# Warm-up matmuls and the order of the first loads in a fused attention and gated-MLP kernel

## The chip, the cores and the metric

The kernel runs on one core of a Trainium2 chip. A core has a matrix engine (TensorE, PE in the profile; its loading of stationary weights is shown as PEld), VectorE (DVE), ScalarE (ACT), GpSimd (POOL) and SyncE (SP), each with an instruction stream of its own, and 16 DMA engines. DMAs are issued by an engine's instruction stream, here SyncE's, GpSimd's and, for a few, ScalarE's; a stream issues in order, and an instruction that has to wait holds everything behind it in that stream. Times are device microseconds (us). The metric is the median time of one execution; lower is better.

## The reference

The input x has 2048 tokens of 512 numbers in bf16. The output is x + s * g: s is an attention block with 32 heads over cached keys and values, g a gated MLP, both fed with the layer-normalized x.

```python
q = (xn @ wq).reshape(B, Sq, H, Dh).transpose(0, 2, 1, 3)
scores = jnp.einsum("bhqd,bhkd->bhqk", q, k_cache) * (Dh ** -0.5)
p = softmax(scores, axis=-1)
o = jnp.einsum("bhqk,bhkd->bhqd", p, v_cache)
s = o.transpose(0, 2, 1, 3).reshape(B, Sq, H * Dh) @ wo

h = gelu(layernorm(xn) @ w1)        # then four column groups shifted by 1, -1, 2, -2 tokens
x1 = xn + shifted(h) @ w2
g = silu(x1 + gelu(layernorm(x1) @ w3) @ w4)
```

H is 32, Dh 128, and there are 2048 cached keys for each head.

## The kernel before, in words

The tokens are handled as 16 tiles of 128, and the attention as 512 units: for each group of four heads, for each of four blocks of 512 queries, for each head of the group. A unit has eight steps; step n is slot n % 8 of unit n // 8. In a slot TensorE multiplies two chunks of 128 keys with the 512 queries (`s_slot`), ScalarE takes the exponential of the 128 x 1024 result, and TensorE multiplies the exponentials of an earlier slot, four or more behind, with V (`pv_slot`). Between these stand the q projections of a unit two ahead (`q_mm`, `q_copy`), the output projections, and the MLP's matmuls in small pieces. VectorE adds up the exponentials for the softmax's denominator, copies and normalizes. Every instruction is pinned to program order, so the order of the calls in the code is the order on each engine's stream.

Keys come transposed by the DMA: `load_k` loads a head's keys in four pieces (KSPLIT) of 512 keys, each one transposing DMA on SyncE's queue. `load_v` loads a head's V in two halves of 256 KB, `load_w` a head's 128 KB of query weights, `ln1_load` a token tile of 128 KB. The layer norm of a token tile takes statistics (`ln1_stats`, VectorE and two GpSimd instructions), the normalizing (`ln1_apply`, VectorE) and a transpose into xnT (`ln1_turn`, a transposing DMA on SyncE's queue). Tiles 0 to 3 go another way: `first_stats` and `first_tokens` normalize them and turn them on TensorE with the identity matrix, make the first queries, and make the first two key pieces' scores in halves, before the loop over the steps begins at step 4.

What stands ahead of `first_tokens` sets the start-up (lines 799 to 815): four token tiles on SyncE's and ScalarE's queues, query weights of heads 0 to 2 on GpSimd's, head 0's keys and V and head 1's keys on SyncE's, then `warm_up`, which multiplies the identity matrix by itself WARM times into a PSUM tile that nothing reads, while the first tokens arrive. Head 3's weights, token tiles 4 to 7 and head 1's V are issued on GpSimd's queue, and two of head 2's key pieces on SyncE's.

Later loads are put into a table by step with `at(n, fn)`; a step's entries run at the end of the step, in the order in which they were entered. Lines 816 to 830 hold those of the start: for each token tile from 4 on the steps of its statistics, its normalizing and its transpose; the rest of the keys of heads 2 and 3 and the V of head 3 on SyncE's queue; and the V of head 2 at steps 3 and 4 on GpSimd's. The transposed tiles 4 to 7 are first read by `q_mm` of unit 4 at step 22 (line 888). The sums of the early units go through a small DRAM tile on SyncE's queue too (`recip`, `bcast`: dr and rb).

Of the kernel before, what the change touches and what calls it, by code (L numbers as in the profile page):

```python
# [17 lines left out]
def kernel(  # L18
# [15 lines left out]
    nc = tc.nc  # L34
    P = nc.NUM_PARTITIONS
# [15 lines left out]
    HG = 4 if H % 4 == 0 else (2 if H % 2 == 0 else 1)  # L51
# [4 lines left out]
    KSPLIT = 4  # L56
# [1 line left out]
    BASE = 16  # L58
    SHIFT = [1, -1, 2, -2]
    PADW = 32  # L60
    WARM = 48
    PSUM = bass.MemoryType.PSUM
    pin = tc.keep_in_program_order

# [18 lines left out]
    ident = const.tile([P, P], BF16, name="ident")  # L83
# [39 lines left out]
    def mm(out, lhsT, rhs, start, stop):  # L123
        mm_count[0] += out.shape[-1] / 512
        pin(nc.tensor.matmul(out=out, lhsT=lhsT, rhs=rhs, start=start, stop=stop))  # L125
# [6 lines left out]
    def again(t):  # L132
        vn = smp.tile([P, 1], FP32, tag="ve", name="vn")
        var = mv1[t][:, 1:2]
        if t < 4:
            pin(nc.gpsimd.tensor_scalar(out=vn[:], in0=var, scalar1=-EPS, scalar2=None, op0=ALU.add))
            var = vn[:]
        pin(nc.gpsimd.tensor_tensor(out=vn[:], in0=var, in1=rs1[t][:], op=ALU.mult))
        pin(nc.gpsimd.tensor_tensor(out=vn[:], in0=vn[:], in1=rs1[t][:], op=ALU.mult))
        rsqrt(mv1[t][:, 1:2], vn[:])  # L140
# [16 lines left out]
    def at(n, fn):  # L157
        todo[n].append(fn)
# [9 lines left out]
    def load_k(h, pieces):  # L168
        w = Sk // KSPLIT
        for i in pieces:  # L170
            if i == 0:
                kTs[h] = kp.tile([P, Sk], BF16, name="kT")
            pin(nc.sync.dma_start(
                out=kTs[h][:, i * w:(i + 1) * w],
                in_=A_k_cache[0, h, i * w:(i + 1) * w, :], transpose=True))

    def load_v(h, halves, eng=nc.sync):
        v = A_v_cache[0, h].rearrange("(i p j) d -> p i j d", p=P, j=KJ)
        for i in halves:
            if i == 0:  # L180
                vBs[h] = vp.tile([P, KC, Dh], BF16, name="vb")
            ks = slice(i * KSPLIT // 2, (i + 1) * KSPLIT // 2)
            pin(eng.dma_start(
                out=vBs[h].rearrange("p (i j) d -> p i j d", j=KJ)[:, ks], in_=v[:, ks]))

    def load_w(h, eng=nc.sync):
        wqs[h] = wqp.tile([P, DC, Dh], BF16, name="wq_h")
        pin(eng.dma_start(out=wqs[h][:], in_=wq_v[:, :, h * Dh:(h + 1) * Dh]))
# [217 lines left out]
    def ln1_load(t, eng):  # L406
        xin = tokp.tile([P, D], BF16, tag="ta", bufs=6, name="xin")
        pin(eng.dma_start(out=xin[:], in_=xsrc[t]))
        ln[t] = xin

    def ln1_stats(t):
        xin = ln[t]
        bn = smp.tile([P, nc.vector.BN_STATS_DIM], FP32, name="bn")
        pin(nc.vector.bn_stats(out=bn[:], in_=xin[:]))
        pin(nc.vector.bn_aggr(out=mv1[t][:], in_=bn[:]))
        rsqrt(rs1[t][:], mv1[t][:, 1:2])
# [44 lines left out]
    def ln1_apply(t):  # L461
        xns[t] = ln1_norm(t)

    def ln1_turn(t):
        pin(nc.sync.dma_start_transpose(out=xnT[:, :, t * P:(t + 1) * P], in_=xns.pop(t)[:]))

    def warm_up(n):
        wt = psS.tile([P, 2, 512], FP32, name="ps_s")
        for _ in range(n):
            mm(wt[:, 0, 0:P], ident[:], ident[:], True, True)  # L470

    def first_tokens(xns):
        ps = [psX.tile([P, 512], FP32, tag=tag, name="ps_q") for tag in ("xa", "xm")]
# [326 lines left out]
        ln1_load(t, eng)  # L800
    act1 = const.tile([P, 1], FP32, name="act1")
    pin(nc.scalar.activation(out=act1[:], in_=nhalf[:, 0:1], func=ACT.Identity))
    for h in range(HG - 1):
        load_w(h, nc.gpsimd)
    load_k(0, range(KSPLIT))
    load_v(0, (0, 1))
    load_k(1, range(KSPLIT))
    warm_up(WARM)
    xns_0 = first_stats()
    load_w(HG - 1, nc.gpsimd)  # L810
    for t in range(4, 8):
        ln1_load(t, nc.gpsimd)
    first_tokens(xns_0)
    load_v(1, (0, 1), nc.gpsimd)
    load_k(2, (0, 1))
    tokens = ((2, 6, 7), (5, 9, 11), (8, 12, 13), (11, 13, 14),
              (26, 29, 29), (27, 31, 31), (33, 36, 36), (35, 39, 39),
              (37, 45, 45), (47, 53, 53), (55, 61, 61), (63, 69, 69))
    for t, (stats, apply, turn) in enumerate(tokens, 4):
        if t >= 8:  # L820
            at({11: 24, 12: 25}.get(t, stats - 8), lambda t=t: ln1_load(t, nc.gpsimd))
        at(stats, lambda t=t: ln1_stats(t))
        at(max(apply + 1, 28 + 7 * t), lambda t=t: again(t))
        at(apply, lambda t=t: ln1_apply(t))
        at(turn, lambda t=t: ln1_turn(t))
    for n, load, h, piece in ((2, load_k, 2, 2), (4, load_k, 2, 3), (8, load_k, 3, 0), (11, load_k, 3, 1),
                              (15, load_k, 3, 2), (17, load_k, 3, 3), (18, load_v, 3, 0), (20, load_v, 3, 1)):
        at(n, lambda load=load, h=h, piece=piece: load(h, (piece,)))
    for i in range(2):
        at(3 + i, lambda i=i: load_v(2, (i,), nc.gpsimd))  # L830
    for t in range(4):
        at(30 + 3 * t, lambda t=t: again(t))
    at(28, ph1_load)
# [3 lines left out]
    for g in range(NG - 1):  # L837
        b = (g * QT + QT - 1) * HG
        for hh in range(HG):
            h = (g + 1) * HG + hh  # L840
            for i in range(KSPLIT):
                n = (b - 2 + (2 * hh + i // 2 + (hh > 0))) * SPU + (5, 7)[i % 2]
# [32 lines left out]
    for n in range(NS):  # L875
        u, p = divmod(n, SPU)
# [54 lines left out]
        if p == 6 and wo_box:  # L931
            gg, t = wo_todo.popleft()
# [54 lines left out]
    gg, t = wo_todo.popleft()  # L987
# [16 lines left out]
    gg, t = wo_todo.popleft()  # L1004
# [60 lines left out]
```

## Time and profile before

| What | Before |
|---|---|
| Median of three runs | 1246.61 us (1246.46 to 1247.11) |
| Profiled execution | 1245.84 us |
| Its span, first to last instruction | 1244.0 us |
| TensorE busy | 1238.1 us (100% of the span) |
| ScalarE busy | 1128.5 us (91%) |
| VectorE busy | 1117.1 us (90%) |
| GpSimd busy | 175.3 us (14%) |

In a row of the timeline the first number is the start in microseconds from the span's start, the second how long the row lasts, then come the engine, the source line, the operation, the tiles it writes and reads, the shape and the number of instructions merged into the row. "SPq" and the like are a queue's issues of DMAs, not the transfers. A bracket at the end tells the idle time before the row and what ended it. Busy matmul time includes the pipeline, so neighbouring matmuls overlap and a busy TensorE isn't one that streams without a gap. Matmuls and weight loads of all kinds carry line 125, that of the helper `mm`, so tiles tell them apart: ps_q are query projections, ps_s scores, ps_o products with V.

### The profile page before, as it was taken

What the parts mean: (1) busy time and instruction counts of PE and PEld (TensorE: products, weight loads), DVE (VectorE), ACT (ScalarE), POOL (GpSimd) and SP (SyncE); (2) the same over time, 40 slices, a digit from 0 to 9 for tenths busy, and PEclk for the clock granted to TensorE, in tenths of its full rate; (3) what the DMA queues carried; (4) which work ended last, traced back from release to release, by engine and by line L of the source; (5) the groups of instructions that cost most, each with busy time, mean ns of one, the idle gap of its engine ahead of it and who ended that gap; (6) DMA issues with size and microseconds to landing.
All of it is one profiled execution on the core that took longest, in us unless ns stands there. A gap on an engine that the chain in (4) does not pass through costs nothing.

```text
span 1244.0 us, 16647 instructions
## 1 busy us (share of the span) xinstructions
PE 1238.1 (100%) x5816; PEld 597.8 (48%) x5816; DVE 1117.1 (90%) x1521; ACT 1128.5 (91%) x1284; POOL 175.3 (14%) x301
## 2 busy tenths in 40 slices
PE   9999999999999999999999999999999999999998
PEld 5444444444444444444444444444444444444444
DVE  7999999999999988899988889999888999888998
ACT  8999998888999888899998889998888999988992
POOL 6563003432111000000100000010000000000110
PEclk9999999999999999999999999999999999999999
DMA  9565563665624455233483235724346233552463
GB/s 199 126 114 101 106 140 77 127 128 121 143 67 107 107 102 119 52 93 74 108 147 93 69 77 110 132 76 82 85 98 127 56 89 65 123 145 73 108 150 108
DMA packets 248404, 131.42 MB, mean 106 GB/s; under 512 B 200000, under 2 KB 224960, under 8 KB 248320
## 3 DMA queue, kind: packets, MB, share of 16 engines
q1 hardware_dynamic: 238752, 103.94, 39.7%
q0 software_dynamic: 8992, 25.96, 9.4%
q8 instruction: 45, 0.74, 0.3%
q10 hardware_dynamic: 576, 0.46, 0.1%
q14 instruction: 39, 0.32, 0.1%
HBM read 83.62 MB, written 8.13 MB: 74 GB/s over the span
## 4 chain that ended last, share of the span: by engine, by line
PE 97%; DMA 1%; ACT 1%; DVE 1%; issue 0%; SPq 0%; POOL 0%; ACTq 0%; POOLq 0%
PE ps_s L125 36%; PE ps_o L125 35%; PE ps_m L125 10%; PE ps_q L125 9%; PE ps_wo L125 8%; DMA rb<-dr 1%; ACT pT L222 0%; DMA xnT<-xn 0%; DMA dr<-rc 0%; DVE oT L305 0%; ACT xnT L492 0%; ACT pre L595 0%; DVE sm L276 0%; DVE sq L562 0%; DVE acc L233 0%
## 5 line engine op out<-in xcount | busy, mean ns | idle before, releaser
L222 ACT ACTIVATE pT<-ps_s 128x1024 bf16<-128x1024 f32 x1020 | 1020.7, 1029 | 89.7 <-PE ps_s L125 75.6
L125 PE MATMUL ps_s<-qT,kT 128*128 128x512 bf16 (+1 forms) x2056 | 609.1, 378 | 0.1
L125 PE MATMUL ps_o<-pT,vb 128*128 128x512 bf16 x2048 | 607.4, 379 | 0.0
L125 PEld LDWEIGHTS <-kT 128*128 128x128 bf16 x2056 | 232.5, 113 | 226.1 <-issue 1.4
L233 DVE TENSOR_TENSOR acc<-acc,pT 128x2048 bf16<-128x2048 bf16 x256 | 310.5, 1213 | 15.2 <-ACT pT L222 14.5
L125 PEld LDWEIGHTS <-vb 128*128 128x128 bf16 x2048 | 200.2, 98 | 225.5
L228 DVE TENSOR_TENSOR acc<-pT 128x2048 bf16<-128x2048 bf16 x128 | 156.2, 1220 | 31.7 <-ACT pT L222 31.2
L125 PE MATMUL ps_q<-xnT,wq_h 128*128 128x512 bf16 (+1 forms) x524 | 152.8, 374 | 1.1 <-DMA xnT<-xn 0.8
L125 PE MATMUL ps_wo<-wo_h,oT 128*128 128x512 bf16 (+1 forms) x460 | 135.1, 377 | 0.0
L305 DVE TENSOR_TENSOR oT<-ps_o,rb 128x512 bf16<-128x512 f32 x122 | 130.8, 1072 | 2.0 <-DMA rb<-dr 1.8
L391 DVE TENSOR_TENSOR s_acc<-ps_wo,s_acc 128x512 f32<-128x512 f32 x96 | 66.1, 688 | 42.2 <-PE ps_wo L125 41.9
L237 DVE TENSOR_TENSOR acc<-acc 128x1024 bf16<-128x1024 bf16 x128 | 87.5, 684 | 0.3
L276 DVE TENSOR_REDUCE sm<-accT 128x4 f32<-128x512 bf16 x122 | 82.8, 678 | 0.5 <-DMA accT<-acc 0.5
L125 PEld LDWEIGHTS <-wq_h 128*128 128x128 bf16 x524 | 50.7, 98 | 60.6 <-DMA xnT<-xn 1.3
L208 DVE CAST qT<-ps_q 128x512 bf16<-128x512 f32 x109 | 74.9, 688 | 3.9 <-PE ps_q L125 3.6
L125 PE MATMUL ps_m<-xn2T,w_sb 128*128 128x512 bf16 x224 | 77.1, 379 | 0.0
L125 PE MATMUL ps_m<-w_sb,h2T 128*128 128x512 bf16 x224 | 77.1, 379 | 0.0
L727 POOL DMA_DIRECT2D w_sb<-in_B_w_dram x28 | 21.2, 756 | 371.9 <-PE ps_m L125 337.7
L125 PEld LDWEIGHTS <-oT 128*128 128x128 bf16 x468 | 45.7, 98 | 54.3 <-DVE oT L312 0.3
L755 POOL DMA_DIRECT2D g_d<-xr x16 | 8.8, 548 | 438.0 <-DVE xr L753 438.0
L238 DVE TENSOR_TENSOR acc<-acc 128x512 bf16<-128x512 bf16 x128 | 54.4, 425 | 4.4
L554 DVE SCALAR_TENSOR_TENSOR sq<-sq,pre 128x1024 bf16<-128x1024 bf16 x36 | 44.0, 1221 | 4.3 <-ACT sq L550 4.3
(103 smaller groups left out, 638.4 us busy)
## 6 DMA issues: line engine op xcount, KB each, us to landing
rb<-dr SPq DMA_DIRECT2D x127, 256.0 KB, 3.7
vb<-in_A_v_cache_dram SPq DMA_DIRECT2D x60, 256.0 KB, 3.9
w_sb<-in_B_w_dram POOLq DMA_DIRECT2D x28, 256.0 KB, 4.3
wo_h<-in_A_wo_dram SPq DMA_DIRECT2D x32, 128.0 KB, 3.6
wq_h<-in_A_wq_dram SPq DMA_DIRECT2D x28, 128.0 KB, 3.3
kT<-in_A_k_cache_dram SPq DMA_TRANSPOSE x128, 3.7
dr<-rc SPq DMA_DIRECT2D x128, 2.0 KB, 2.1
xr<-in_A_x_dram POOLq DMA_DIRECT2D x16, 128.0 KB, 3.2
```

The lines of the kernel that those rows point to most:

```text
L125: pin(nc.tensor.matmul(out=out, lhsT=lhsT, rhs=rhs, start=start, stop=stop))
L208: pin(nc.vector.tensor_copy(out=qT[:], in_=st[u].pop("psq")[:]))
L222: pin(nc.scalar.activation(out=s["pT"][-1][:, jj:jj + 2, :], in_=sps[:], func=ACT.Exp, scale=SCALE))
L228: pin(nc.vector.tensor_tensor(out=s["acc"][:], in0=s["pT"][0][:], in1=s["pT"][1][:], op=ALU.add))
L233: pin(nc.vector.tensor_tensor(out=a[:], in0=a[:], in1=st[u]["pT"][i][:], op=ALU.add))
L237: pin(nc.vector.tensor_tensor(out=a[:, 0:2, :], in0=a[:, 0:2, :], in1=a[:, 2:4, :], op=ALU.add))
L238: pin(nc.vector.tensor_tensor(out=a[:, 0, :], in0=a[:, 0, :], in1=a[:, 1, :], op=ALU.add))
L276: pin(nc.vector.tensor_reduce(out=sm[:], in_=s.pop("at")[:], axis=mybir.AxisListType.X, op=ALU.add))
L305: pin(nc.vector.tensor_tensor(out=oTs[(g, qt)][:, hh, :].rearrange(f, j=4), in0=s["o"].rearrange(f, j=4), in1=s["rb"].rearrange("x (p j) - ...
L391: pin(nc.vector.tensor_tensor(out=sa, in0=ps[:], in1=sa, op=ALU.add))
L554: pin(nc.vector.scalar_tensor_tensor(out=sq[:].rearrange(f2), in0=sq[:].rearrange(f2), scalar=1.0, in1=pre[:].rearrange(f2), op0=ALU.add, ...
L727: pin(nc.gpsimd.dma_start(out=w[:], in_=w3_v[:, :, fc * P:(fc + 2) * P]))
```

## The change

The warm-up becomes 12 matmuls of the identity with a moving operand of 512 columns (the identity four times over, by a broadcast access). Query weights of heads 1 and 2 move from GpSimd's queue to SyncE's, between head 0's key pieces. Head 1's V moves from GpSimd's queue to SyncE's, its halves between and behind head 1's key pieces. Token tile 7's load moves from the start to step 3, behind tile 4's statistics on GpSimd's queue, and tile 6's behind `first_tokens` in program order. Head 2's V moves from steps 3 and 4 to steps 6 and 9, behind the statistics of tiles 5 and 6. The second key piece of head 3 moves from step 11 to step 14, behind tile 7's transpose.

```diff
-    WARM = 48
+    WARM = 12
...
         for _ in range(n):
-            mm(wt[:, 0, 0:P], ident[:], ident[:], True, True)
+            mm(wt[:, 0, :].rearrange("p (a b) -> p a b", a=4), ident[:],
+               ident[:].unsqueeze(1).broadcast_to([P, 4, P]), True, True)
...
-    for h in range(HG - 1):
-        load_w(h, nc.gpsimd)
-    load_k(0, range(KSPLIT))
+    load_w(0, nc.gpsimd)
+    load_k(0, (0, 1))
+    for h in range(1, HG - 1):
+        load_w(h)
+        load_k(0, (h + 1,))
     load_v(0, (0, 1))
-    load_k(1, range(KSPLIT))
+    for i in range(2):
+        load_k(1, (2 * i, 2 * i + 1))
+        load_v(1, (i,))
     warm_up(WARM)
     xns_0 = first_stats()
     load_w(HG - 1, nc.gpsimd)
-    for t in range(4, 8):
+    for t in range(4, 6):
         ln1_load(t, nc.gpsimd)
     first_tokens(xns_0)
-    load_v(1, (0, 1), nc.gpsimd)
+    ln1_load(6, nc.gpsimd)
     load_k(2, (0, 1))
...
-        if t >= 8:
-            at({11: 24, 12: 25}.get(t, stats - 8), lambda t=t: ln1_load(t, nc.gpsimd))
+        if t >= 7:
+            at({11: 24, 12: 25}.get(t, max(stats - 8, 2)), lambda t=t: ln1_load(t, nc.gpsimd))
...
-    for n, load, h, piece in ((2, load_k, 2, 2), (4, load_k, 2, 3), (8, load_k, 3, 0), (11, load_k, 3, 1),
+    for n, load, h, piece in ((2, load_k, 2, 2), (4, load_k, 2, 3), (8, load_k, 3, 0), (14, load_k, 3, 1),
...
     for i in range(2):
-        at(3 + i, lambda i=i: load_v(2, (i,), nc.gpsimd))
+        at(6 + 3 * i, lambda i=i: load_v(2, (i,), nc.gpsimd))
```

## The prediction

> **What bounds the kernel now.** I read the page's head and its chain of waits first. The profiled execution took 1245.84 us, 1.84 us more than its span; the median of the three runs shown is 1246.61, so what I work out as a difference in the span is put on 1246.61.
>
> ```profile
> span 1244.0 us, 16647 instructions
> PE 97%; DMA 1%; ACT 1%; DVE 1%; issue 0%; SPq 0%; POOL 0%; ACTq 0%; POOLq 0%
> ```
>
> TensorE carries 97% of the chain. The change touches loads and warm-up before the steady state, so only idle time near the start can be won. Stretches of 5 us and one of 18 us show where it is; after the time come PE, PEld, DVE, ACT and POOL busy, then granted clock, DMA share and GB/s:
>
> ```profile
> 5.00:10.00 5.00, 4.72 (x55) 4.09 (x54) 3.25 (x10) 3.52 (x8) 4.76 (x9) 1.00 1.11 183
> 12.50:30.50 18.00, 17.95 (x89) 8.37 (x87) 16.40 (x28) 18.00 (x20) 10.77 (x15) 1.00 1.09 204
> 30.00:35.00 5.00, 4.19 (x20) 1.78 (x18) 3.45 (x5) 3.55 (x5) 0.00 (x0) 1.00 0.73 143
> ```
>
> From 12.5 to 30.5 us both ScalarE (18.00 of 18.00) and TensorE are full and the DMA engines are over 100% booked. Between 30 and 35 us TensorE loses 0.81 us and ScalarE is idle as well. The timelines of these two engines and the chain of waits name the cause:
>
> ```profile
> 29.85 0.59 PE L125 MATMUL ps_o<-pT,vb 128*128 128x512 bf16 x2
> 31.26 0.60 PE L125 MATMUL ps_q<-xnT,wq_h 128*128 128x512 bf16 x2 [0.81 <-DMA xnT<-xn]
> 32.33 1.95 ACT L222 ACTIVATE pT<-ps_s 128x1024 bf16<-128x1024 f32 x2 [1.16 <-PE ps_s L125]
> 28.06 3.16 DMA xnT<-xn
> ```
>
> The q matmul of the second 512 tokens needs token tiles 4 to 7 transposed (xnT). Tile 7's transpose is issued at 28.06 and lands at 31.22; TensorE was ready at 31.26 - 0.81 = 30.45. ScalarE's gap of 1.16 is longer than TensorE's 0.81, so a recovered stall isn't simply swallowed by a busy ScalarE. That 0.81 us is the only DMA wait of any size in the start-up, and the stake of the change. Why is the transpose so late? SyncE's own timeline, all rows up to it (start, time, operation):
>
> ```profile
> 1.65 5.13 SPq L173 DMA_TRANSPOSE kT<-in_A_k_cache_dram  x4
> 6.82 1.09 SPq L183 DMA_DIRECT2D vb<-in_A_v_cache_dram  x2
> 7.96 12.82 SPq L173 DMA_TRANSPOSE kT<-in_A_k_cache_dram  x8
> 20.89 1.22 SPq L465 DMA_TRANSPOSE xnT<-xn  x1
> 22.16 1.26 SPq L173 DMA_TRANSPOSE kT<-in_A_k_cache_dram  x1
> 23.52 1.21 SPq L465 DMA_TRANSPOSE xnT<-xn  x1
> 24.77 1.26 SPq L173 DMA_TRANSPOSE kT<-in_A_k_cache_dram  x1
> 26.13 0.52 SPq L263 DMA_DIRECT2D dr<-rc  x1
> 26.75 2.54 SPq L465 DMA_TRANSPOSE xnT<-xn  x2
> ```
>
> SyncE issues without a pause from 1.65 to 29.3, so its queue, not the data, makes tile 7 late: four key pieces take 5.13 (1.28 each), but the eight from 7.96 take 12.82 where 8 x 1.28 = 10.26 would do. Those 2.56 us of stretched issue fall where the DMA engines are overbooked; I call what is left of them after the change S.
>
> **The change, part by part.** *SyncE's queue.* Added ahead of tile 7's transpose: two query-weight loads and the second head's V in two pieces. Taken from ahead of it: one key piece of head four (step 11 to 14, now behind the transpose of tile 7). Rows for a SyncE weight issue (min/median/max) and the V pair above:
>
> ```profile
> L188 SPq DMA_DIRECT2D wq_h<-in_A_wq_dram x28: 426/526/587, 86.1 to 1042.3; - x28
> DMA to landing us min/median/max: 3.2/3.7/4.1
> ```
>
> Added: 2 x 0.53 + 2 x 0.55 = 2.15 us. Removed: the key piece from 24.77 to the next issue at 26.13, 1.36 us. So tile 7's transpose is issued at 28.06 - 2.56 + S + 2.15 - 1.36 = 26.29 + S. The second row above is the landing time of the four xnT transposes, median 3.7: landing at 29.99 + S against a need at 30.45, so the stall is S - 0.46, and nothing below S = 0.46.
>
> *POOL's queue.* Its rows, and landing medians by queue up to 40 us:
>
> ```profile
> 1.35 2.43 POOL L188 DMA_DIRECT2D wq_h<-in_A_wq_dram  x3 [0.28 <-issue]
> 7.67 2.15 POOL L408 DMA_DIRECT2D xin<-in_A_x_dram  x4
> 9.82 1.43 POOL L183 DMA_DIRECT2D vb<-in_A_v_cache_dram  x2
> 16.02 1.51 POOL L183 DMA_DIRECT2D vb<-in_A_v_cache_dram  x2
> 18.95 0.99 POOL L130 TENSOR_TENSOR rs<-ve,nhalf 128x1 f32<-128x1 f32 x1
> vb<-in_A_v_cache_dram POOLq DMA_DIRECT2D x4, 256.0 KB, 6.8
> xin<-in_A_x_dram POOLq DMA_DIRECT2D x9, 128.0 KB, 4.6
> ```
>
> S comes from here. POOL's loads issued between 6.8 and 17.6 us are one weight tile, four token tiles and four V pieces: 128 + 4 x 128 + 4 x 256 = 1664 KB, in flight beside the eight stretched key pieces. The change takes the second head's V off this queue, holds the third head's until after token tile 5's and tile 6's statistics, and leaves tile 7 in the same stretch, about 16 us: only weights and tiles 4 to 6, 512 KB, are left beside the eight keys before that, 31%. S is bounded by 0 (the stretch was POOL's traffic alone) and 2.56 (it belongs to SyncE's own transposes). As an estimate I scale with the bytes: 0.31 x 2.56 = 0.79, nearer to 0, because SyncE's first four key pieces show no stretch while POOL had only the three weight tiles out. The stall is then 0.79 - 0.46 = 0.33 and the gain 0.81 - 0.33 = 0.48 us.
>
> The Trainium skill (DMA: Bandwidth & Descriptors, "Issuing engines are not separate DMA queues") says that all issuing queues end on the same 16 engines, and that spreading issues only saves sequencer time. By that rule the move saves no transfer and only lengthens SyncE's issue, S stays at 2.56 and the time would be the first rival's. The same page ("SWDGE vs HWDGE vs iDMA") says that GpSimd's loads need descriptors that VectorE's two-port mode can lock out, and SyncE's don't; by that one S is 0 and the whole 0.81 comes back. Between them only the run decides; that the stretch sits at 8 to 21 us and not before speaks for the second.
>
> *Loads that move to where they could be late.* Each is costed at nothing, with its cover:
>
> ```profile
> 9.24 0.82 PE L125 MATMUL ps_q<-xnT,wq_h 128*128 128x128 bf16 x6
> 11.20 0.59 PE L125 MATMUL ps_q<-xnT,wq_h 128*128 128x512 bf16 x2
> 12.96 0.59 PE L125 MATMUL ps_o<-pT,vb 128*128 128x512 bf16 x2
> vb<-in_A_v_cache_dram SPq DMA_DIRECT2D x4, 256.0 KB, 4.2
> kT<-in_A_k_cache_dram SPq DMA_TRANSPOSE x1, 5.3
> DMA to landing us min/median/max: 2.4/3.4/5.9
> 21.00 0.69 DVE L414 BATCH_NORM_STATS2 bn<-xin 128x6 f32<-128x512 bf16 x1
> 23.87 0.41 DVE L449 TENSOR_SCALAR xn<-xin,mv,rs 128x512 bf16<-128x512 bf16 x1 [0.46 <-POOL rs L130]
> 27.98 0.59 PE L125 MATMUL ps_o<-pT,vb 128*128 128x512 bf16 x2
> DMA to landing us min/median/max: 3.1/5.4/9.2
> ```
>
> Head one's query weights take SyncE's third place, issued at 1.65 + 2 x 1.28 = 4.21, needed at 9.24 + 4 x 0.056 = 9.46. The key piece issued in that place took 5.3 (9.51, 0.05 late); weight loads over the whole run take 2.4 to 5.9 with median 3.4 (7.6; at worst 10.1, 0.65 late). Two of three weight loads that shared the DMA engines then have left POOL's queue, so I take the earlier side: no cost. Head two's follow 0.53 + 1.28 = 1.8 us later for a matmul at 11.20, 1.7 later: the same answer. The first V, now issued 2 x 0.53 later at 7.88, has 12.96 - 7.88 = 5.1 us where SyncE's V loads took 4.2.
>
> Tile 7's load leaves at about 16.0 on POOL (where the V pair stood) instead of some 9.3, and is read by the statistics at 21.00: 16.0 + 4.6 = 20.6 is in time, with V's 6.8 it is 22.8, and VectorE waits 1.8. Queued behind that wait are unit 0's reciprocal, unit 1's first sum and the tile's own normalizing, now done at 23.87 + 0.41 = 24.28 and then at 26.1 at the latest: still before SyncE gets to its transpose at 26.29 + S. No cost; SyncE's queue is the cover.
>
> The third head's V is issued after POOL's rs at 19.94; landing 3.1 to 9.2 later (23.0 to 29.1), first read at 27.98: at worst 1.1 late, with the median 6.8 on time by 1.2. No cost.
>
> *Warm-up.* Twelve matmuls of 512 columns replace 48 of 128, the same 6144 columns.
>
> ```profile
> 1.39 5.17 PE L125 MATMUL ps_s<-ident 128*128 128x128 bf16 x48 [1.39 <-DVE ident L87]
> 6.40 0.61 PE L125 MATMUL ps_o<-ident,xn 128*128 128x128 bf16 x8
> 5.28 0.81 ACT L442 ACTIVATE xn<-xin,nb,rsA 128x512 bf16<-128x512 bf16 x1
> ```
>
> The 48 start one per 107 ns until shortly before their end, the eight behind them one per 56 ns: half rate, then full rate, though the clock column says 1.00 at once. Twelve wide ones at half rate take 12 x 4 x 107 = 5.1 us, at full rate 12 x 216 = 2.6 us; if the full rate comes at the same moment, they end where the 48 did. The first token tile is ready at 6.09, so an earlier end wins at most 0.31 and a wholly slow one costs 0.1. I take 0.
>
> **Sum.** -0.48 + 0 + 0 = -0.48 us: 1246.61 - 0.48 = 1246.1 us.
>
> **The rivals.** *SyncE becomes the bound (slower).* S stays 2.56: landing at 32.55, stall 2.10, 1.29 more than now: 1247.9. Decides from S = 0.46 + 0.81 = 1.27. For it: the pure issue time ahead of tile 7 grows by 0.79. Against it: the stretch began only with POOL's V and tokens in flight.
> *A new wait instead.* The third head's V lands at 29.1: TensorE waits 1.1 at step 20, which hides the old wait behind it: 1246.61 - 0.81 + 1.1 = 1246.9. For it: 9.2 is the longest row of that tile. Against: the longest was queued behind other loads.
> *The change doesn't do what it says.* Tile 7's wait stays 0.8, because landing rather than issue grew: 1246.6.
> *The clock rises later.* If the wide warm-up doesn't bring full rate by 6.4, the matmuls up to 9.24 (some 2.5 us of busy time) take twice as long: 1249.1. Against: the same columns stream without a gap.
>
> **How the numbers follow.** Forecast (S between 0 and 1.27, 1245.8 to 1246.6): 0.62. SyncE bound 0.16, new wait 0.08, unchanged 0.09, clock 0.05. The range reaches from 1245.1 (whole stall gone, 0.31 of the warm-up, and 0.4 for the scatter, the three runs shown being 0.65 apart) to 1248.0 (SyncE's full stretch); its own part for the forecast is 1245.6 to 1246.8. A measurement of this kernel can tell about 0.2% (2.5 us) from no change. Faster by that much would need more than every idle stretch of the start: 0.02. Slower by that needs the late clock, or S above 3.8: 0.05. Within: 0.93.
>
> **What would show it.** Right: the wait before ps_q at step 22 shrinks from 0.81 to 0.3 or goes, SyncE's key issues run near 1.28 each, tile 7's transpose is issued near 27.1, the first exponential of step 4 starts as before. Wrong: key issues stretched as now; a wait on wq_h near 9.5, on vb near 28, or on xn before the transpose; more than two matmuls at half rate after the warm-up.

## The result, and the profile after

| What | Before | After |
|---|---|---|
| Median, both on one chip | 1245.85 us (1244.76 to 1247.11, 17 runs) | 1248.17 us (1246.63 to 1251.26, 17 runs) |
| Ratio after / before | | 1.0021, 95% interval 1.0014 to 1.0027 |
| Profiled execution | 1245.84 us | 1246.63 us |
| Its span | 1244.0 us | 1244.9 us |

The change makes the kernel about 2.3 us slower. The forecast was 1246.1, so it missed by 2.1 us, with the wrong sign. One thing has to be kept in mind with every profile below: single executions of one kernel lie up to 4.6 us apart here, and the profiled execution of the changed kernel is the fastest of its 17. It shows where the change begins to cost, not the whole of the median's 2.3 us.

SyncE's timeline of the changed kernel, the rows ahead of tile 7's transpose that answer to those of before (start, time, line, operation):

```profile
1.65 2.52 SPq L173 DMA_TRANSPOSE kT<-in_A_k_cache_dram  x2
4.21 0.58 SPq L188 DMA_DIRECT2D wq_h<-in_A_wq_dram  x1
4.84 1.19 SPq L173 DMA_TRANSPOSE kT<-in_A_k_cache_dram  x1
6.07 0.58 SPq L188 DMA_DIRECT2D wq_h<-in_A_wq_dram  x1
6.69 1.19 SPq L173 DMA_TRANSPOSE kT<-in_A_k_cache_dram  x1
7.93 1.09 SPq L183 DMA_DIRECT2D vb<-in_A_v_cache_dram  x2
9.06 2.45 SPq L173 DMA_TRANSPOSE kT<-in_A_k_cache_dram  x2
11.55 0.58 SPq L183 DMA_DIRECT2D vb<-in_A_v_cache_dram  x1
12.18 2.45 SPq L173 DMA_TRANSPOSE kT<-in_A_k_cache_dram  x2
14.67 0.58 SPq L183 DMA_DIRECT2D vb<-in_A_v_cache_dram  x1
15.30 5.68 SPq L173 DMA_TRANSPOSE kT<-in_A_k_cache_dram  x4
...
25.65 2.53 SPq L465 DMA_TRANSPOSE xnT<-xn  x2
```

The stretched issue of the keys is gone but for the last four pieces (5.68, where 4 x 1.28 is 5.12). The second transpose of the last row is tile 7's; the chain of waits gives its issue as 26.96. So S, the stretch that the prediction had left open, comes out as 26.96 - 26.29 = 0.67 us if it is read off the moment of that issue. Read off the rows it is smaller: the eight key pieces behind the first V take 2.45 + 2.45 + 5.68 = 10.58, which is 0.32 over the prediction's 10.26, where it allowed 0.79. The four added issues take more than was allowed, 2.51 instead of 2.15 (0.63 from the start of each to that of the next row, 0.62 for one). The two misses cancel but for 0.11. What came of it, in the chain of waits around it (start, time, piece):

```profile
26.16 0.79 DVE acc L233
26.96 4.13 DMA xnT<-xn
31.09 0.25 issue
31.34 0.59 PE ps_q L125 x2
```

The transpose is issued 1.10 us earlier than before (28.06), but takes 4.13 us to land where it took 3.16: it arrives at 31.09, only 0.13 us earlier. TensorE waits 0.64 instead of 0.81, but it also reaches the wait later (31.34 - 0.64 = 30.70 instead of 30.45), and the matmul behind it starts at 31.34, 0.08 us later than before. GpSimd's timeline shows what shares the DMA engines with the transpose, one row of five token loads, 640 KB. The kernel before has the same row, the first of these two; there the transpose follows 4.27 us behind it, here 2.94:

```profile
23.79 2.76 POOL L408 DMA_DIRECT2D xin<-in_A_x_dram  x5
24.02 2.76 POOL L408 DMA_DIRECT2D xin<-in_A_x_dram  x5
```

The same stretches of time as before (after the time: PE, PEld, DVE, ACT and POOL busy, granted clock, DMA share, GB/s):

```profile
5.00:10.00 5.00, 4.65 (x42) 3.16 (x41) 2.83 (x10) 3.11 (x8) 4.05 (x7) 1.00 0.86 163
12.50:30.50 18.00, 18.00 (x91) 8.61 (x88) 16.11 (x27) 18.00 (x21) 9.73 (x16) 1.00 1.07 210
30.00:35.00 5.00, 4.36 (x21) 1.88 (x19) 3.64 (x5) 3.74 (x5) 0.00 (x0) 1.00 1.10 175
```

Between 5 and 10 us the DMA engines are booked 0.86, where they were booked 1.11 and moved 183 GB/s; afterwards they are as full as before (1.07 against 1.09), and between 30 and 35 us they still are (1.10 against 0.73). The last column says the same in bytes: fewer are moved from 5 to 10 us (163 against 183 GB/s), more from 30 to 35 (175 against 143). In this profile transfers have moved to a later time.

And there is a wait that was not there before, at step 46, near 55 us. The chain of waits of the changed kernel leads through the sums of unit 3 (of 128 units, 8 groups of heads by 4 blocks of queries by 4 heads; 512 is the number of queries in a block), which go to DRAM and back on SyncE's queue (rc is VectorE's reciprocal, dr the 2 KB tile in DRAM, rb its return):

```profile
46.74 0.16 DVE rc L261
...
46.92 4.34 DMA dr<-rc
...
51.31 3.54 DMA rb<-dr
...
54.88 0.70 DVE oT L312
...
55.63 0.39 PE ps_wo L125
```

In the kernel before, SyncE's timeline has the same two issues closer together, 2.46 us instead of 4.39 apart:

```profile
48.01 0.38 SPq L263 DMA_DIRECT2D dr<-rc  x1
...
50.47 0.33 SPq L295 DMA_DIRECT2D rb<-dr  x1
```

dr is issued 1.09 us earlier than before, but rb comes back at 54.85 (51.31 + 3.54), and VectorE's product oT, which needs it, starts 0.69 us later than before; TensorE's output projection waits for oT. VectorE's timeline before, and TensorE's after:

```profile
54.19 0.69 DVE L312 TENSOR_TENSOR oT<-ps_o,rb 128x512 bf16<-128x512 f32 x1 [0.28 <-DMA rb<-dr]
```

```profile
55.63 0.39 PE L125 MATMUL ps_wo<-wo_h,oT 128*128 128x512 bf16 x1 [0.44 <-DVE oT L312]
```

The prediction's reading ended at step 22; nothing in it looked at this round trip.

### The profile page after: what moved, and what is told of

It reads as the page before. It is cut to its first block, busy times and chain, and to the rows that moved or that the text cites. A ratio compares the mean times of both kernels' runs of the same rounds, so it can differ in the third digit from the quotient of the medians.

```text
span 1244.9 us, 16570 instructions
## 1 busy us (share of the span) xinstructions
PE 1238.4 (99%) x5780; PEld 594.8 (48%) x5780; DVE 1116.7 (90%) x1521; ACT 1127.9 (91%) x1284; POOL 170.1 (14%) x297
## 4 chain that ended last, share of the span: by engine, by line
PE 96%; DVE 1%; DMA 1%; ACT 1%; POOL 0%; issue 0%; POOLq 0%; SPq 0%
PE ps_s L125 35%; PE ps_o L125 34%; PE ps_m L125 10%; PE ps_q L125 9%; PE ps_wo L125 8%; DVE acc L233 0%; ACT pT L222 0%; DMA dr<-rc 0%; DMA xnT<-xn 0%; DMA rb<-dr 0%; DVE bn L414 0%; ACT xnT L493 0%; DVE acc L237 0%; DVE qT L208 0%; DVE oT L312 0%
```

## The experiments

Eighteen kernels, each timed beside the kernel before on the same chip. The expectations name theories by letters. W: the wide warm-up moves the clock's rise. L: the order of the loads. Within L, D: the loads that come later (tile 7, third head's V, key piece); Q: SyncE's queue, which gets four loads more, runs later; O: the sums of unit 3 at step 46. A, F, R, I are explained where they come.

### Warm-up or order

`narrow_warm_new_order` is the changed kernel with 48 narrow warm-up matmuls, `wide_warm_old_order` the kernel before with 12 wide ones.

Against the changed kernel, the first:

```diff
-    WARM = 12
+    WARM = 48
...
-            mm(wt[:, 0, :].rearrange("p (a b) -> p a b", a=4), ident[:],
-               ident[:].unsqueeze(1).broadcast_to([P, 4, P]), True, True)
+            mm(wt[:, 0, 0:P], ident[:], ident[:], True, True)
```

The second is the same edit the other way round, against the kernel before.

> The changed order of loads with the old warm-up of 48 matmuls of 128 columns. Theory W (the wide warm-up costs the time, by the clock of TensorE rising later or falling again): within 0.5 us of before, and the single runs as close together as those of before (2.4 us from lowest to highest). Theory L (the order of the loads costs it): 2 us and more slower than before, like the changed kernel, with single runs up to 5 us apart. If both have a part: 0.7 to 1.5 us slower.

> The old order of loads with the new warm-up of 12 matmuls of 512 columns. Theory W: 1.5 to 2.5 us slower than before, with runs up to 5 us apart and a mean granted clock under 1.000 in the slowest of them. Theory L: within 0.5 us of before.

Measured, against a median of 1246.12 for the kernel before: the new order with the old warm-up 1247.82 us (ratio 1.0012, 1.0003 to 1.0021); the old order with the new warm-up 1246.79 (1.0004, 0.9995 to 1.0013). The order alone is slower, the warm-up alone can't be told from no change. L holds in the main and W falls as the only cause. The third case, that both have a part, is not excluded by these two: the order alone costs 1.5 to 1.7 us, less than the 2.3 of the whole change.

The changed kernel once more, and with 16 wide matmuls instead of 12:

```diff
-    WARM = 12
+    WARM = 16
```

> The changed kernel unaltered, on the same chip as the two mixtures. Both theories: about 2.3 us slower than before; its second profile shows whether the start-up of the first one is typical. Theory W: a profiled execution that is slower than 1246.6 us shows the slow matmuls of the start lasting longer than to 6.9 us. Theory L: it shows longer waits for DMAs between 9 and 60 us.

> The changed kernel with 16 wide warm-up matmuls instead of 12. Theory W with the clock rising too late: the four more keep TensorE busy until it has risen, and the time falls by 0.5 to 1.5 us against the changed kernel. Theory W with the clock falling again after the warm-up, and theory L: no gain, and up to 0.9 us (4 x 216 ns) to 1.7 us (4 x 427 ns) more.

Measured: 1249.41 (1.0028, 1.0017 to 1.0039) and 1249.11 (1.0024, 1.0015 to 1.0033). The four extra matmuls only start the first tokens later: the warm-up lasts to 7.5 instead of 6.7 us. More useful is the profile of `changed_again`, at 1249.27 a typical execution of the changed kernel. Its wait for tile 7 is gone, and the wait at step 46 is 2.05 us (chain of waits):

```profile
47.98 3.69 DMA dr<-rc
...
51.73 3.81 DMA rb<-dr
...
56.32 0.39 PE ps_wo L125
```

Behind it the granted clock falls (same columns as above; the clock is the number ahead of the DMA share):

```profile
56.95:60.36 3.41, 3.41 (x9) 1.22 (x8) 3.38 (x7) 2.02 (x2) 0.00 (x1) 0.50 0.20 38
```

For 3.41 us TensorE runs at half its clock and loses up to half of that, 1.7 us, in addition to the wait. Six of the seven executions of `changed_again` and six of the 17 of the changed kernel have a mean granted clock of 0.999 or less, against 6 of 133 of the kernel before in the five groups of runs. 3.41 us at half is 1.7 in 1248, a mean of 0.9986: that is the size seen. The count is rough all the same: the profile of `only_to_sync` (below) has 0.999 too, and its only half clock begins at 1244.63 us, behind TensorE's last work.

### Which part of the order

`only_to_sync`, against the kernel before:

```diff
-    for h in range(HG - 1):
-        load_w(h, nc.gpsimd)
-    load_k(0, range(KSPLIT))
+    load_w(0, nc.gpsimd)
+    load_k(0, (0, 1))
+    for h in range(1, HG - 1):
+        load_w(h)
+        load_k(0, (h + 1,))
...
-    load_k(1, range(KSPLIT))
+    for i in range(2):
+        load_k(1, (2 * i, 2 * i + 1))
+        load_v(1, (i,))
...
-    load_v(1, (0, 1), nc.gpsimd)
```

`only_later`, against the kernel before:

```diff
-    for t in range(4, 8):
+    for t in range(4, 7):
...
-        if t >= 8:
-            at({11: 24, 12: 25}.get(t, stats - 8), lambda t=t: ln1_load(t, nc.gpsimd))
+        if t >= 7:
+            at({11: 24, 12: 25}.get(t, max(stats - 8, 2)), lambda t=t: ln1_load(t, nc.gpsimd))
...
-    for n, load, h, piece in ((2, load_k, 2, 2), (4, load_k, 2, 3), (8, load_k, 3, 0), (11, load_k, 3, 1),
+    for n, load, h, piece in ((2, load_k, 2, 2), (4, load_k, 2, 3), (8, load_k, 3, 0), (14, load_k, 3, 1),
...
-        at(3 + i, lambda i=i: load_v(2, (i,), nc.gpsimd))
+        at(6 + 3 * i, lambda i=i: load_v(2, (i,), nc.gpsimd))
```

> The kernel before with one part of the change: query weights of heads 1 and 2 and the second head's V on SyncE's queue; token tile 7, the third head's V and the key piece of head 3 stay where they were. Theory Q (the four loads on SyncE's queue cost it): 1 to 2 us slower than before, with the wait for tile 7 near 30 us at 1.5 us or more, since the key piece still stands ahead of it. Theory D (the loads put later cost it): within 0.5 us of before. Theory O (in the new order everything on SyncE's queue from 36 us on runs a microsecond early, so that w1 and the output weights fill the DMA engines ahead of the fourth unit's sums, and TensorE waits for oT at 55 us): as Q in time, but by a wait of 0.4 us or more at 55 us.

> The kernel before with the other part: token tile 7's load at step 3, the third head's V at steps 6 and 9, the key piece of head 3 at step 14; weights and the second head's V stay on POOL's queue. Theory D: 1 to 2 us slower than before. Theory Q: no slower than before, and the wait for tile 7 is under 0.5 us, so up to 0.8 us faster. Theory O: the wait for tile 7 shrinks, but the wait for oT at 55 us shows in its place, 0 to 1 us slower.

Measured, against 1246.16: the four loads on SyncE's queue 1248.59 (1.0023, 1.0014 to 1.0032), the later loads 1246.17 (1.0003, 0.9995 to 1.0012). The whole loss lies in the loads that moved to SyncE's queue; D falls.

Then each of the two pairs by itself, the edits being the two halves of `only_to_sync`:

> The kernel before, with the V of head 1 alone on SyncE's queue between head 1's key pieces (1.1 us of issue). If each of the four moved loads counts alike (theory Q: SyncE's queue runs later by the sum of the issues), half of the 2.4 us that the four together cost: 1.0 to 1.5 us above the kernel before. If the loss hangs on the place in the DMA stream at which the fourth unit's sums meet the wo burst (theory O): either no loss (within 0.5 us) with the oT wait at step 46 under 0.3 us, or the full 2 us with the wait at 0.4 or more.

> The kernel before, with the query weights of heads 1 and 2 alone on SyncE's queue between head 0's key pieces (1.05 us of issue). Theory Q: 1.0 to 1.5 us above the kernel before. Theory O: either no loss (within 0.5 us) with the oT wait at step 46 under 0.3 us, or the full 2 us with the wait at 0.4 or more.

Measured, against 1246.32: V alone 1246.68 (1.0002, 0.9993 to 1.0011), the weights alone 1249.28 (1.0018, 1.0009 to 1.0027). Both add the same time of issue, 1.1 us, to the same queue, and only one costs, 2.2 us by the ratio and 3.0 by the medians; Q, by which each counts alike, falls in this form. In the profile with the weights alone the time is lost at the start (TensorE's timeline):

```profile
14.56 0.61 PE L125 MATMUL ps_o<-pT,vb 128*128 128x512 bf16 x2 [1.79 <-DMA vb<-in_A_v_cache_dram]
...
19.30 0.62 PE L125 MATMUL ps_s<-qT,kT 128*128 128x512 bf16 x2 [1.33 <-DMA kT<-in_A_k_cache_dram]
...
21.92 0.62 PE L125 MATMUL ps_s<-qT,kT 128*128 128x512 bf16 x2 [0.48 <-DMA kT<-in_A_k_cache_dram]
```

The first V is needed at 12.77 and comes at 14.5. The chain of waits of this kernel shows a key piece in flight for 11.62 us:

```profile
10.26 11.62 DMA kT<-in_A_k_cache_dram
```

The opposite edit, the changed kernel with only the weights put back (theory A: they are the whole loss):

```diff
-    load_w(0, nc.gpsimd)
-    load_k(0, (0, 1))
-    for h in range(1, HG - 1):
-        load_w(h)
-        load_k(0, (h + 1,))
+    for h in range(HG - 1):
+        load_w(h, nc.gpsimd)
+    load_k(0, range(KSPLIT))
```

> The changed kernel, with the query weights of heads 1 and 2 back on GpSimd's queue at the start; all else as changed (wide warm-up, the second head's V on SyncE's queue, tile 7, the third head's V and the key piece later). Theory A (the two weight issues on SyncE's queue are the whole loss, as the last batch suggests, where V alone cost nothing and the weights alone 2.4 us): within 0.5 us of the kernel before, 1245.7 to 1246.8, first V landed by 11.9, no half clock. Rival (the loss needs the new order as a whole, any two of its parts cost it): 1247.5 or more.

Measured, against 1246.08: 1246.66 (1.0003, 0.9994 to 1.0012). A holds: with the weights back on GpSimd's queue all the rest of the change costs nothing that can be told. One edit removed takes the loss away, the same edit alone brings it.

### Step 46: is it the burst of output weights

In the changed kernel dr (2 KB) takes 4.34 us behind four loads of output weights on the same queue. In the kernel before it stands behind the same four and rb is issued 2.46 us later. Two kernels move these loads away from there, one behind the sums and one far ahead of them; two more try the same on the kernel before, with some other transfers moved as well.

`changed_wo_behind_sums`, against the changed kernel (`changed_wo_early` has step 20 for 38):

```diff
-        at(31 + h, lambda h=h: load_wo(h))
+        at(38, lambda h=h: load_wo(h))
```

`before_tidied`, against the kernel before (`before_wo_early_tidied` has step 20 for 38):

```diff
-        at(31 + h, lambda h=h: load_wo(h))
+        at(38, lambda h=h: load_wo(h))
...
-            at({11: 24, 12: 25}.get(t, stats - 8), lambda t=t: ln1_load(t, nc.gpsimd))
+            at({11: 24, 12: 25}.get(t, stats - 8), lambda t=t: ln1_load(t, nc.sync if 10 <= t <= 12 else nc.gpsimd))
...
-    for n, load, h, piece in ((2, load_k, 2, 2), (4, load_k, 2, 3), (8, load_k, 3, 0), (11, load_k, 3, 1),
+    for n, load, h, piece in ((2, load_k, 2, 2), (4, load_k, 2, 3), (8, load_k, 3, 0), (14, load_k, 3, 1),
```

> The changed kernel with the four output-weight loads of the first group at step 38 instead of 31 to 34, behind the fourth unit's sums on SyncE's queue; the weights are first read at step 44. Theory O: the wait for oT at 55 us and the half clock behind it go, 1 to 2 us faster than the changed kernel. Theories Q and D: the time stays that of the changed kernel, since the cost lies before 40 us.

> The kernel before with three moves of its own: the output weights at step 38, the key piece of head 3 at step 14, and token tiles 10 to 12 on SyncE's queue instead of POOL's, so that they no longer share the DMA engines with tile 7's transpose. Theory O: both waits (tile 7's 0.8 us at 30 us, and the one for oT in the slower runs) go, 0.8 to 1.5 us faster than before and with single runs closer together. Theories Q and D: at most tile 7's 0.8 us faster.

> The changed kernel, with the first group's four output-weight loads (wo) at step 20 instead of steps 31 to 34, so that they leave SyncE's queue before the fourth unit's sums are sent through it. Theory O (the changed kernel loses because the sums' transfer dr and its return rb stand behind w1 and the wo burst on SyncE's queue, and TensorE then waits for oT at step 46, in some runs with the clock falling to half after it): the wait of ps_wo on oT at step 46 is under 0.2 us (0.4 and 2.1 in the two profiles of the changed kernel), no half clock near 57 us, median 1.0 to 2.0 us below the changed kernel's, about 1246.5 to 1247.3. Theory Q (four more loads on SyncE's queue cost by their place at the start alone: tile 7's wait and the issue time): the wait may go but the median stays at the changed kernel's, 1248.0 to 1249.0, 2 us or more above the kernel before.

> The kernel before, with the wo loads of the first group at step 20, the second key piece of head 3 at step 14 and token tiles 10 to 12 loaded on SyncE's queue instead of GpSimd's. Theory O (waits for tile 7's transpose and for oT are what can be won at the start): tile 7's wait (0.8 us before) is under 0.2, no wait on wo, no wait above 0.3 on oT, median 0.8 to 1.3 us below the kernel before, about 1245.0. Rival (what is won at one wait reappears at the next load, as in the first tidied kernel): another DMA wait of 0.8 us or more in the first 60 us, median within 0.5 us of before or above it.

Measured: `changed_wo_behind_sums` 1248.45 (1.0018, 1.0009 to 1.0027); the wait for oT is gone, and one of 0.7 us for the output weights themselves stands in its place, so it decides nothing. `before_tidied` 1247.64 (1.0011, 1.0002 to 1.002): tile 7's wait is gone, but the output weights come 1.3 us late. `changed_wo_early` 1247.1 (1.0002, 0.9993 to 1.0011): within O's range, and no longer to be told from the kernel before although the query weights are still on SyncE's queue; but not for O's reason. Its profile still waits 0.7 us for oT, and 2.3 us for V, and its chain of waits still has the slow round trip, with no output weights near it:

```profile
48.07 4.43 DMA dr<-rc
...
52.55 3.68 DMA rb<-dr
```

So the burst isn't what makes dr slow, and O, in the form that the output weights stand in its way, falls. Why the median is better all the same stays open.

What goes with the slow dr can be seen in windows behind its issue (same columns; the last number, GB/s, is the one to read): the changed kernel, `changed_wo_early`, and the kernel before:

```profile
47.50:48.75 1.25, 1.25 (x8) 0.55 (x6) 1.25 (x3) 1.25 (x2) 1.17 (x3) 1.00 0.17 11
```

```profile
49.25:51.00 1.75, 1.75 (x10) 0.75 (x9) 1.72 (x5) 1.75 (x3) 1.50 (x6) 1.00 0.45 23
```

```profile
48.00:49.25 1.25, 1.25 (x7) 0.59 (x6) 1.22 (x4) 1.25 (x3) 1.17 (x4) 1.00 1.04 301
```

For 1.25 and 1.75 us the DMA engines together move almost nothing while dr is outstanding; that is most of the 1.9 and 2.0 us by which the two dr (4.34 and 4.43) are slower than in the kernel before (2.4). Such standstills are not special to the changed order: `wide_warm_old_order` has one too (63 GB/s from 47.0 to 49.5 us, and a wait of 0.8 us for oT), and the kernel before has one at a place where no matmul waits (59 GB/s from 13.9 to 15.5 us). What causes them stays open.

`before_wo_early_tidied` is a telling miss. In its profile TensorE waits for no DMA at all between 9 and 62 us, and yet its median, 1246.81 against 1246.32 (1.0002, 0.9993 to 1.0011), is no better than that of the kernel before. ScalarE's timelines show where part of the gain goes in this execution, the first row from the kernel before and the second from this one:

```profile
100.42 0.69 ACT L595 ACTIVATE pre<-ps_m,mv 128x512 bf16<-128x512 f32 x1 [0.20 <-POOL vn L138]
```

```profile
100.16 0.69 ACT L595 ACTIVATE pre<-ps_m,mv 128x512 bf16<-128x512 f32 x1 [0.67 <-POOL vn L138]
```

The MLP's normalization has a chain of its own through GpSimd; ScalarE reaches it earlier and waits 0.47 us longer. Another 0.8 us is lost between 600 and 900 us, where TensorE waits for an oT. That no part of the 0.81 us can be won is not shown: this kernel moves other loads too, and the interval of its ratio reaches from 0.9 us faster to 1.4 slower.

### How do the weights cost it

Theory F: they make the first V late (needed at 12.96 before; SyncE now issues it 1.1 us later). Theory R: the loss is further on, wherever the first V stands. Two kernels put the first V ahead of head 0's last key piece: `weights_v_first`, otherwise like `only_wq_to_sync`, and `changed_v_first`, otherwise like the changed kernel. The edit is the same:

```diff
-    for h in range(1, HG - 1):
-        load_w(h)
-        load_k(0, (h + 1,))
-    load_v(0, (0, 1))
+    load_w(1)
+    load_k(0, (2,))
+    load_w(2)
+    load_v(0, (0, 1))
+    load_k(0, (3,))
```

> The kernel before, with the query weights of heads 1 and 2 on SyncE's queue as in the change, but the first V ahead of head 0's last key piece, so that it is issued near 6.7 us as before the change instead of near 7.9. Theory F (the weights cost because the first V comes later: needed at 12.96, landed at 12.2 to 14.5 in the eight profiles with the weights on SyncE's queue, at 10.3 to 11.7 in the six without): first V landed by 12.0, no wait for V near 13 us, median within 0.7 us of the kernel before. Theory R (they cost further on, through the fourth unit's sums at step 46 and the half clock behind it, wherever the first V stands): the wait of ps_wo on oT at step 46 is still 0.4 or more and the median still 1.5 to 3 us above.

> The changed kernel with the first V ahead of head 0's last key piece. Theory F: 1.3 to 2.3 us below the changed kernel, 1246.0 to 1247.0, no wait for V near 13 us. Theory R: unchanged, 1248.0 to 1249.4, with the wait on oT at step 46.

Measured, against 1246.08: 1250.89 (1.0035, 1.0022 to 1.0049) and 1250.92 (1.0032, 1.0021 to 1.0044), both worse than without the swap. F's forecast of a gain falls; but V's share is not separated by this edit, since it puts head 0's last key piece 1.1 us later in V's stead. In the first kernel V is in time and the keys are late instead (TensorE's timeline, then the window behind the second wait):

```profile
16.13 0.62 PE L125 MATMUL ps_s<-qT,kT 128*128 128x512 bf16 x2 [1.76 <-DMA kT<-in_A_k_cache_dram]
...
22.19 0.69 PE L125 MATMUL ps_s<-qT,kT 128*128 128x512 bf16 x2 [2.00 <-DMA kT<-in_A_k_cache_dram]
```

```profile
22.62:26.03 3.41, 3.41 (x9) 1.21 (x8) 0.45 (x2) 2.05 (x2) 3.15 (x7) 0.50 1.18 279
```

R falls too as it was put: the first of the two kernels has no wait for oT at step 46 at all (the second one of 0.7 us). The loss is not tied to one place.

Theory I: it is SyncE's issue time. `two_small_issues` leaves the weights on GpSimd's queue and puts two small loads of 512 rows of 16 bytes where the change has the weights:

```diff
-    load_k(0, range(KSPLIT))
+    load_k(0, (0, 1))
+    for h in range(1, HG - 1):
+        pin(nc.sync.dma_start(out=xnT[:, :, Sq - h * P:Sq - h * P + 8], in_=wq_v[:, :, h * Dh:h * Dh + 8]))
+        load_k(0, (h + 1,))
```

> The kernel before, its weights on GpSimd's queue, and at the two places between head 0's key pieces where the change issues the weights two small loads of the same form on SyncE's queue (512 rows of 16 bytes instead of 256 each; nothing reads them before they are overwritten), 0.6 us of issue each. Theory I (the price is SyncE's issue time, which makes all behind it later by 1.1 us): 1.5 to 3 us above the kernel before, first V issued near 7.9 and landed after 12.2. If the price is that of the weights themselves on this queue (their bytes, or their place in the DMA engines' order): within 0.7 us of the kernel before.

Measured: 1248.05 (1.0019, 1.001 to 1.0027): by the ratio 16 KB cost as much as the weights' 256 KB, so a loss of this size does not need the weights' bytes. That both lose by the same way is not shown. SyncE's timeline shows that the price here wasn't pure issue time either; a key piece behind the small loads took 2.72 us to issue, where 1.2 would do, and the first V is issued at 9.47, not near 7.9:

```profile
6.08 0.58 SPq L807 DMA_DIRECT2D xnT<-in_A_wq_dram  x1
6.71 2.72 SPq L173 DMA_TRANSPOSE kT<-in_A_k_cache_dram  x1
9.47 1.09 SPq L183 DMA_DIRECT2D vb<-in_A_v_cache_dram  x2
```

Last, 1.1 us of other issues taken off SyncE's queue: the first V goes to ScalarE's, in the changed kernel and in the one before.

```diff
     pin(nc.scalar.activation(out=act1[:], in_=nhalf[:, 0:1], func=ACT.Identity))
+    load_v(0, (0, 1), nc.scalar)
...
-    load_v(0, (0, 1))
```

> The changed kernel with the first V's two halves on ScalarE's queue, issued right at the start, so that SyncE's issues from the last key piece of head 0 on come 1.1 us earlier and no later than in the kernel before, with the weights still at their places. Theory I (the loss is the 1.1 us of issue that the weights put ahead of head 0's V and of all the keys behind it on SyncE's queue): the loss goes, 1246.0 to 1247.0, half clock in at most one run of ten. Rival (it is the weights' place between head 0's own keys, ahead of the third and fourth piece, which stays): 1248.0 to 1249.4 as the changed kernel.

> The kernel before with the first V's two halves on ScalarE's queue: SyncE's queue 1.1 us earlier from 6.8 us on, the mirror image of what the change did to it. If theory I held in both directions, tile 7's wait (0.81) would go and the median fall by 0.5 to 1.0 us, to 1245.1 to 1245.7. If the start-up only loses by lateness and a gain is taken back later (at 100 us in the traces without waits at the start): within 0.4 us of the kernel before. If V, now in flight with the first key pieces, makes these late: 1 us or more above it.

Measured, against 1246.05: 1249.81 (1.003, 1.0018 to 1.0042) and 1247.64 (1.0016, 1.0007 to 1.0025). Both are slower, so the mirror image of the change wins nothing. But in neither is SyncE's queue earlier, so theory I's condition isn't met and they do not test it; they show that issue times don't simply add up. In the second the twelve first key pieces take 19.50 us in one row, where they took 5.13 + 12.82 before, and TensorE waits 1.7 us for tile 7 and 0.4 for keys, which is the third of the cases expected. In the first, SyncE gains no time, since a key piece among the early ones now takes 1.95 us to issue, and tile 7's transpose is issued at 27.33 and lands after 5.74 us (timelines of SyncE and TensorE, then the chain of waits and the window behind it):

```profile
4.84 1.95 SPq L173 DMA_TRANSPOSE kT<-in_A_k_cache_dram  x1
```

```profile
33.32 0.59 PE L125 MATMUL ps_q<-xnT,wq_h 128*128 128x512 bf16 x2 [2.38 <-DMA xnT<-xn]
```

```profile
27.33 5.74 DMA xnT<-xn
```

```profile
34.13:37.54 3.41, 3.41 (x9) 1.22 (x8) 2.18 (x3) 2.05 (x2) 0.00 (x0) 0.50 1.00 204
```

### What fits, and what stays open

One number seemed to part the kernels, the DMA share from 7 to 10 us. The windows of before, V alone on SyncE's queue, the weights alone, and the changed kernel:

```profile
7.00:10.00 3.00, 2.72 (x32) 2.16 (x31) 1.40 (x3) 2.31 (x5) 3.00 (x6) 1.00 1.13 197
```

```profile
7.00:10.00 3.00, 2.89 (x34) 2.39 (x34) 1.53 (x3) 2.32 (x5) 2.87 (x5) 1.00 1.05 222
```

```profile
7.00:10.00 3.00, 2.89 (x34) 2.36 (x32) 1.35 (x3) 2.32 (x5) 3.00 (x6) 1.00 0.90 145
```

```profile
7.00:10.00 3.00, 2.65 (x36) 2.19 (x34) 0.99 (x3) 2.20 (x5) 2.17 (x4) 1.00 0.82 142
```

With the weights between head 0's keys on one queue the share is 0.82 and 0.90 just before a stretch of 20 us in which it averages over 1; with the weights on GpSimd's queue beside the keys it is 1.13 and 1.05. The reading would be that about 0.25 of 3 us of all engines' time, 0.7 us, is not used and can't be made up before 30 us, and some transfer then comes late. The record speaks against it. The share counts the whole time of a packet (one piece of a transfer) in the window in which the packet begins, also while it stands still, and so is not bytes moved. In GB/s the kernels do not part: `only_later` and `wide_warm_old_order`, which cost nothing that can be told, move 145 and 169 GB/s in this window, `weights_v_first` and `changed_v_first`, which cost most, 194 and 205. And from 0 to 30 us the changed kernel and the kernel before move the same 201 GB/s. `changed_v_on_scalar` (1.32, 214 GB/s) loses 3.8 us with full engines; `two_small_issues` (1.19, 98 GB/s) has the share of the fast kernels and fewer bytes than any.

Shown is which edit costs the time: the weights alone bring the loss, and without them it is gone. It costs only beside the rest of the schedule as it is, for with the output weights loaded at step 20 the loss can't be told either. How it costs stays open. Neither a late first V alone (`changed_again` waits for none) nor a simple sum of issue times explains it. That the transfer that pays (V, keys, tile 7, the sums) differs from one execution to the next would fit the standstills, which fall at other places in each profile; that is argued, not shown.

## Why the prediction was wrong

*What bounds the kernel* was read rightly. Whether the stake of 0.81 us could be won is doubtful: with no DMA wait left at the start (`before_wo_early_tidied`) no median gain was measured, part of it being taken back at 100 us in that profile.

*SyncE's queue.* Tile 7's transpose was issued at 26.96 against 27.08 forecast, in part by luck: the key pieces' stretch was 0.32 and not 0.79, the added issues 2.51 and not 2.15. That the stretch would mostly go was right. The scaling by bytes is not borne out; it also left out that head 1's V, 512 KB, stays in flight beside these keys, from the other queue. Of the two rules of the Trainium skill that were weighed there (DMA: Bandwidth & Descriptors), the one on GpSimd's descriptors, which VectorE can lock out and SyncE's DMAs don't need ("SWDGE vs HWDGE vs iDMA"), was put down for S = 0, and 0.32 is nearer to that than to 2.56. That is no support for it: it speaks of GpSimd's own loads and not of SyncE's issue times, and no run here shows its mechanism.

*The landing of 3.7* was the first term that was mis-sized. It measured 4.13 in the changed kernel's profile, and 5.74 in `changed_v_on_scalar`. The median of four landings was used as if the time of landing didn't depend on what else is in flight; the earlier transpose meets GpSimd's five token loads at 24.02. Of the 0.48 us forecast for this wait, 0.17 came, and as TensorE reached the wait 0.25 us later, the matmul behind it was no earlier at all. In `changed_again` the wait is gone, and the median is still slower.

*Loads that move to where they could be late: "each is costed at nothing".* This is the step that failed. For the later loads, and for V on SyncE's queue, nothing was right within what can be told (1246.17 against 1246.16 and 1246.68 against 1246.32). For the two weight loads it was wrong by the whole result: by themselves they cost 3.0 us by the medians (1249.28 against 1246.32) and 2.2 by the ratio (1.0018). The step asked only whether each moved transfer would itself be in time, with a landing time taken from other conditions. The weights were; in the profile with them alone, the V and the keys behind them on the queue were not. By which way the loss comes in the changed kernel stays open, as said above. The first V had 5.1 us of cover against 4.2: it took 4.73 in the changed kernel (12.66, just in time) and 6.6 in `only_wq_to_sync`, 1.79 late.

*Nothing was costed behind step 22.* The round trip of unit 3's sums at step 46 gave 0.44 us of wait in the changed kernel's profile and 2.05 in the typical one, and the half clock behind such a wait was in no term.

*Warm-up* at nothing was right within what can be told (1246.79 against 1246.12; and 1246.66 against 1246.08 with all of the change but the weights).

*The rivals.* The first had nearly the right time, 1247.9, and its point of decision (S of 1.27) was never reached: a right size by luck, with another mechanism. The Trainium skill's rule beside it, that all issuing queues end on the same 16 engines ("Issuing engines are not separate DMA queues", same page), agrees with the result so far that none of these eighteen kernels has a median below that of the kernel before; why one move costs 2.2 us or more and another nothing, it does not tell. "A new wait instead" was right in kind and wrong in place. A slow clock did come, but in the middle of the work, behind a wait, and not after the warm-up.

## What to carry to other kernels

When loads are moved while the DMA engines are booked over 100%, price not only whether each moved load arrives in time, but what stands behind it on its queue. Read the DMA share together with GB/s; the share alone misled here. Follow every DMA round trip on the same queue well past the stage that the change is aimed at, to the first place where a gain is taken back. Undo one edit and do it alone before believing in any single wait: here each profile showed another one, and only the pair of medians named the edit. And before a cause is called refuted, check in the trace that the edit did what it was made for: two kernels meant to make SyncE's queue earlier did not.

## What the runs showed of the hardware

A wait of TensorE in the middle of the work can cost more than itself. Behind waits of 2.00, 2.05 and 2.38 us the granted clock was 0.50 for 3.41 us, beginning 0.4 to 0.8 us after the wait; behind waits of 1.90 (`wide16_new_order`, step 46) and 1.79 us it stayed at 1.00. Five waits do not make a threshold. As an estimate from these rows, a wait of 2.00 us costs up to 2.00 + 1.7 = 3.7.

The time that SyncE takes to issue a transposing load of a key piece is not a constant: 1.2 to 1.3 us in most rows, up to 2.72 where the DMA share was over 1, so an issue time from a quiet stretch is a lower bound.

A load's landing time says more about what is in flight than about the load: a key piece took 5.3 us where the third one stood in the kernel before, and one issued at 10.26 took 11.62 in `only_wq_to_sync`. Even the 2 KB of dr took 4.34 us.

The DMA engines as a whole can come almost to a standstill with transfers outstanding: 11 GB/s for 1.25 us in the changed kernel, 23 for 1.75 in `changed_wo_early`, 46 from 14.25 to 17.00 us in `only_wq_to_sync`, where a key piece in flight took 11.62 us. No run here shows the cause.
